# Storing the rows of a streamed weight chunk interleaved in DRAM

## The chip, the cores and the metric

One core of a Trainium2 chip runs the whole program. The metric is the device time of one execution in microseconds (us), median of several runs. Runs over 1.5% above the fastest of their kernel are marked slow.

## The reference, cut to what matters

The program computes two independent parts and puts them side by side. Part A is a long convolution by FFT; it fills most of the first 460 us and does not matter here. Part B is attention with a recurrent memory: 64 segments of 32 tokens, one after another, each projected by four weights of 1024 x 4096 (bf16).

```
for s in range(64):
    h = concat([mem, x[s]])                    # 40 rows
    q, k, v = h @ Wq, h @ Wk, h @ Wv           # 32 heads of 128
    o = softmax(mask(q k^T)) v @ Wo
    mem, out[s] = o[:8], o[8:]
```

The weights are 64 chunks of 512 KB. The program keeps 43 of them on the chip; the other 21 are streamed from DRAM again for every segment (two of them are parked elsewhere after the first segment, hence 64 x 19 + 2 = 1,218 loads).

## The kernel before

The streamed chunks are first copied into a DRAM tensor of their own, WS, one row of 4,096 bytes per partition. A ring of six SBUF tiles then receives them. Parts that do not matter are cut (`# ...`).

```python
RING = 6
PITCH = 2048
# ...
    def stream_src(ch):
        return WS[ring_order.index(ch), :, 0:2048]
# ...
    WS = dram.tile([len(ring_order), 128, PITCH], BF, name="WS")
# ...
                t = pw()
                nc.sync.dma_start(t[:], dram_chunk(ch))
                if ch in streamed:
                    nc.gpsimd.dma_start(stream_src(ch), t[:])
# ...
        for ch in ring_order:
            if ch[0] == 3:
                nc.gpsimd.dma_start(dst_view(stream_src(ch), ch), dram_chunk(ch))
# ...
    def slot():
        k = free.pop(0)
        t = ring.tile([128, 2048], BF, tag=f"wring{k}", name="wring")
        return k, t

    def fetch():
        if loads:
            s, ch = loads.pop(0)
            live[s, ch] = k, t = slot()
            nc.sync.dma_start(t[:], stream_src(ch))
```

The matmuls read a ring tile piece by piece; when one is done with, its slot goes back and the next load is issued on SP's queue.

## Time and profile before

| | before |
|---|---|
| time, median of 3 runs | 2193.94 us (2190.12 to 2201.51) |
| span of the profiled run | 2198.0 us |
| stream of weights, first to last issue | 461 to 2,175 us |
| loads of the stream | 1,218 of 512 KB |
| DMA rate in the stream, share of the 16 engines | 388 GB/s, 1.01 |
| 4,096-byte packets of SP's queue, 600 to 2,100 us | mean 168.3 ns, median 162 |
| TensorE waits for the stream | 188.2 us |

In the lines below, PE is TensorE (PEld its weight loads), DVE, ACT and POOL are the vector, scalar and GpSimd engines, and SP is the engine that issues the loads of the stream. A packet is one record of a DMA copy; in the stream it has 4,096 bytes, one row of one partition. The share of the DMA engines is the recorded time of their packets over the time of 16 engines; it can come out a little over 1.

The span is read in two stretches: before and after about 460 us. In the second, the DMA engines are always busy (share 1.01 from 600 to 2,100 us) and TensorE is not (1,213 of these 1,500 us), and what TensorE waits for most is the stream. Two lines of the page, the busy time of each engine and the granted TensorE clock in 40 slices (tenths of full speed):

```profile
PE 1721.9 (78%) x35607; PEld 927.7 (42%) x35636; DVE 884.2 (40%) x2702; ACT 638.6 (29%) x1118; POOL 412.2 (19%) x1103
...
PEclk9889997879999999999999999999999999999999
```

One more view, the tile view of wring, gives SP's time to issue a load (shortest, median, longest, in ns):

```profile
L658 SPq DMA_DIRECT2D wring<-WS x1218: 319/320/2190, 460.6 to 2175.1; - x174
```

### The profile page before, as it was taken

How to read it: one execution, taken by the hardware profiler on the slowest of the kernel's cores; microseconds unless marked ns; L12 is line 12 of the kernel's file. 1: busy time of each engine (PE TensorE's matmuls, PEld its weight loads, DVE VectorE, ACT ScalarE, POOL GpSimd, SP SyncE). 2: the span in 40 equal slices, each digit the busy share in tenths (PEclk: the TensorE clock that was granted, in tenths of full speed). 3: DMA queues.
4: the chain of work that ended last, by engine and by line, in shares of the span. 5: the costliest groups of instructions: out<-in, count | busy, mean ns of one | idle time of the engine just before them, and what ended most of it. 6: DMA issues, size and time to landing. Idle time of an engine off the chain costs nothing. (4 is left out here: it accounts for less than half of the span.)

```text
span 2198.0 us, 81500 instructions
## 1 busy us (share of the span) xinstructions
PE 1721.9 (78%) x35607; PEld 927.7 (42%) x35636; DVE 884.2 (40%) x2702; ACT 638.6 (29%) x1118; POOL 412.2 (19%) x1103
## 2 busy tenths in 40 slices
PE   4679975957777788878888888887887878888886
PEld 2233332424444444444444444444444444444444
DVE  8827853123333333333333333333333333333332
ACT  5845530112222222222222222222222222222222
POOL 5004331001111112111111111111111211211111
PEclk9889997879999999999999999999999999999999
DMA  9989989899999999999999999999999999999997
GB/s 322 345 291 342 318 238 325 275 346 390 386 380 378 381 374 390 385 378 395 391 392 395 391 393 393 392 397 365 396 392 387 394 390 376 388 392 388 390 385 273
DMA packets 294286, 807.80 MB, mean 368 GB/s; under 512 B 84940, under 2 KB 84972, under 8 KB 293927
## 3 DMA queue, kind: packets, MB, share of 16 engines
q1 hardware_dynamic: 263592, 738.36, 89.0%
q0 software_dynamic: 23536, 50.51, 6.8%
q10 hardware_dynamic: 6800, 13.72, 1.7%
q8 instruction: 279, 4.57, 0.9%
q14 instruction: 79, 0.65, 0.1%
HBM read 743.06 MB, written 62.39 MB: 366 GB/s over the span
## 5 line engine op out<-in xcount | busy, mean ns | idle before, releaser
L806 PEld LDWEIGHTS <-rec 128*32 128x32 bf16 x12351 | 324.2, 96 | 471.6 <-issue 255.0
L806 PE MATMUL acc<-wring,rec 128*32 128x512 bf16 (+1 forms) x3777 | 374.7, 385 | 136.0 <-DMA wring<-WS 122.1
L815 ACT CAST qkv_sb<-acc 128x512 bf16<-128x512 f32 x384 | 224.8, 585 | 676.2 <-PE acc L806 645.7
L806 PE MATMUL acc<-Wres,rec 128*32 128x512 bf16 x4864 | 394.9, 383 | 1.5 <-issue 1.4
L892 PEld LDWEIGHTS <-OT 128*32 128x32 bf16 x8192 | 217.8, 96 | 178.1 <-issue 151.6
L892 PE MATMUL yacc<-Wlate,OT 128*32 128x256 bf16 x5120 | 221.8, 274 | 13.0 <-issue 11.9
L892 PE MATMUL yacc<-wring,OT 128*32 128x256 bf16 x3072 | 153.9, 276 | 98.5 <-DMA wring<-WS 59.0
L806 PE MATMUL acc<-Wmid,rec 128*32 128x512 bf16 x3072 | 226.1, 383 | 0.5 <-issue 0.5
L752 PEld LDWEIGHTS <-OTB 128*16 128x16 bf16 x4096 | 104.5, 89 | 103.9 <-issue 94.0
L878 ACT CAST OT<-OTp 128x512 bf16<-128x512 f32 x128 | 74.9, 585 | 241.4 <-PE OTp L870 241.3
L707 POOL DMA_DIRECT2D rec<-REC x64 | 37.4, 584 | 566.6 <-issue 268.9
L908 DVE COPY KT<-tps 128x512 bf16<-128x512 bf16 x64 | 27.2, 424 | 289.1 <-PE tps L821 289.1
L879 DVE CAST OTB<-OTp 128x128 bf16<-128x128 f32 x128 | 37.3, 291 | 258.6 <-ACT OT L878 258.6
L647 DVE TENSOR_SCALAR wring<-OTp 128x384 int32<-128x384 int32 x126 | 112.2, 890 | 61.5 <-PE acc L806 54.2
L752 PE MATMUL SB<-Wlate,OTB 128*16 128x256 bf16 x2480 | 98.0, 277 | 35.4 <-DVE SB L743 19.3
L782 POOL COPY KT<-rec 128x128 bf16<-128x128 bf16 x128 | 38.6, 302 | 439.2 <-PE SB L830 430.9
L836 DVE TENSOR_REDUCE mx<-SB 128x5 f32<-128x200 f32 x128 | 47.1, 368 | 182.8 <-PE SB L830 182.8
L767 POOL DMA_DIRECT2D out_dram<-YB x128 | 73.1, 578 | 236.4 <-DVE YB L765 212.9
L752 PE MATMUL SB<-wring,OTB 128*16 128x256 bf16 x1488 | 78.8, 274 | 36.5 <-DVE SB L731 30.8
L821 PE MATMUL tps<-ident,qkv_sb 128*128 128x128 bf16 x1024 | 101.2, 221 | 7.8 <-DVE wring L647 0.2
L821 PEld LDWEIGHTS <-qkv_sb 128*128 128x128 bf16 x1024 | 62.7, 97 | 104.7 <-ACT qkv_sb L815 64.4
L556 PE MATMUL kb_ps<-XBT,pw 128*128 128x512 bf16 x314 | 87.7, 400 | 9.3 <-ACT XBT L512 7.6
(214 smaller groups left out, 2300.8 us busy)
## 6 DMA issues: line engine op xcount, KB each, us to landing
wring<-WS SPq DMA_DIRECT2D x1218, 512.0 KB, 7.3
rec<-REC POOLq DMA_DIRECT2D x64, 192.0 KB, 6.0
SK<-s_sb SPq DMA_DIRECT2D x16, 512.0 KB, 4.8
SU<-s_sb SPq DMA_DIRECT2D x16, 512.0 KB, 4.6
Ug<-SU SPq DMA_DIRECT2D x32, 256.0 KB, 6.1
Kg<-SK ACTq DMA_DIRECT2D x32, 256.0 KB, 5.5
REC<-stage SPq DMA_DIRECT2D x4, 2048.0 KB, 15.2
SZ<-zs SPq DMA_DIRECT2D x31, 256.0 KB, 3.0
```

The costliest lines, as they stand in the source:

```text
L556: nc.tensor.matmul(ps[:], lhsT=ws[kc][:, hl * 128:(hl + 1) * 128], rhs=XBT[:, kc].rearrange("p s t -> p (s t)"), start=(kc == 0), stop=(kc ...
L647: nc.vector.tensor_scalar(out=dst, in0=src, scalar1=0, scalar2=None, op0=ALU.bitwise_or)
L707: nc.gpsimd.dma_start(rec[:], REC[:, s, :])
L752: nc.tensor.matmul(self.acc[32 * dq:32 * dq + W, x - o:y - o], lhsT=self.OTB[:, c, 4 * g + i, :], rhs=r, start=first and not self.seeded, ...
L767: nc.gpsimd.dma_start(bass.AP(outb.tensor, outb.offset + (SEG * NB * self.b + NX) * 2048 + 256 * dq, [[2048 * SEG, NB], [2048, 8], [1, 256 ...
L782: nc.gpsimd.tensor_copy(KT[:, :, :, 32:40], KBs[:, 128 * g:128 * g + 128].rearrange("p (c i t) -> p i c t", c=4, i=4))
L806: nc.tensor.matmul(self.acc[32 * c:32 * c + 32, x - 512 * c:y - 512 * c], lhsT=hT[:, kc, :], rhs=r, start=(kc == 0 and x == 512 * c), stop ...
L815: nc.scalar.copy(sb[:], self.acc[:])
L821: nc.tensor.transpose(tp[:, i * 128:(i + 1) * 128], sb[:, i * 128:(i + 1) * 128], ident[:])
L836: nc.vector.tensor_reduce(out=mx[:], in_=S, op=ALU.max, axis=AX.X)
L878: nc.scalar.copy(OT[:], o_view[:, :, :, 0:32])
L892: nc.tensor.matmul(yacc[32 * dq:32 * dq + 32, x - o:y - o], lhsT=OT[:, c, i, :], rhs=r, start=(h == 0 and x == o), stop=(h == 31), tile_po ...
```

## The change

The intent: row `hi*8 + lo` is stored at place `lo*16 + hi`, so that the 16 rows with the same `lo` are neighbours in DRAM. That such an order is read faster was the assumption.

```diff
     def stream_src(ch):
-        return WS[ring_order.index(ch), :, 0:2048]
+        return WS[ring_order.index(ch), :, 0:2048].rearrange("(lo hi) c -> hi lo c", hi=16)
...
             if ch[0] == 3:
-                nc.gpsimd.dma_start(dst_view(stream_src(ch), ch), dram_chunk(ch))
+                for hh in range(2):
+                    nc.gpsimd.dma_start(stream_src(ch)[:, :, hh * 1024:(hh + 1) * 1024],
+                                        dram_chunk(ch)[:, hh, :].rearrange("(hi lo) d -> hi lo d", hi=16))
```

So the load of a chunk goes from 128x2048 to a source of 16x8x2048. Bytes, packets, matmuls and ring are the same.

## The prediction

The sum came to 3,660, 3,340 and 2,930 us; the packet times behind the first and the last are cut, and only 285 ns, from the early load X_sb, is left: 2,777 + 481 + 80 = 3,338 us. The prediction took 3,300 us, leaning to the upper half, and gave 86% to a slowdown, to between 2,500 and 3,700 us. Of the rivals, the first is that the new order is read faster, the second that nothing changes.

> **What bounds the kernel now.** I read the page's slices first. Up to slice 8 of 40 (about 460 us) the stages are mixed; from there to the end the pattern repeats for 64 segments, and DMA is at 9 tenths throughout.
>
> ```profile
> DMA  9989989899999999999999999999999999999997
> GB/s 322 345 291 342 318 238 325 275 346 390 386 380 378 381 374 390 385 378 395 391 392 395 391 393 393 392 397 365 396 392 387 394 390 376 388 392 388 390 385 273
> ```
>
> Second, the windows view of the steady part, cut into pieces. Columns: stretch, length, busy of PE, PEld, DVE, ACT, POOL with counts, granted clock, DMA share, GB/s. PE is busy 81%, the DMA engines all the time, at 388 GB/s.
>
> ```profile
> 600.00:2100.00 1500.00, 1212.78 (x29764) 691.69 (x29767) 544.52 (x1960) 385.02 (x729) 265.25 (x840) 0.99 1.01 388
> 900.00:1200.00 300.00, 242.35 (x5975) 140.10 (x5967) 108.11 (x388) 75.93 (x144) 55.34 (x174) 0.99 1.01 389
> ```
>
> Third, the waits of TensorE and what is issued. The streamed chunk wring<-WS (512 KB, 128 rows of 4,096 bytes, 1,218 times) is what the matmuls wait for, in the two lines below and in the chain of waits, where wring<-WS has 11% of the span, more than any other entry.
>
> ```profile
> PE acc L806 <- DMA wring<-WS: 122.1, 276, 2.0
> PE yacc L892 <- DMA wring<-WS: 59.0, 110, 1.6
> wring<-WS SPq DMA_DIRECT2D x1218, 512.0 KB, 7.3
> ```
>
> The tile view of wring puts the wait of PE for these landings at 188.2 us in all. 1,218 chunks of 524,288 bytes are 639 MB of the 808 MB moved. So the stream, 461 us to 2,175 us (first to last issue), is paced by DMA; SP often waits for a ring slot only because the 6 slots are all in flight or in use (a landing takes 7.3 us, over five chunks of the 1.41 us that one costs: 1,500 us / 1,064 chunks issued in the window above).
>
> Fourth, the DMA packet records (queue, start, duration, bytes). Between 600 and 2,100 us there are 136,186 packets of 4,096 bytes on SP's queue: quartile 159 ns, median 162, mean 168.3, 99th percentile 360. Packets of 2,048 bytes earlier have a floor of 84 ns. Two sizes give about 75 ns per 2,048 bytes and 9 ns fixed. Hence the **most that a better order of reading can give**: (168.3 - 159) x 136,186 / 16 = 79 us in that window, about 91 us for the whole stream, 4% of the time.
>
> [...] After the change the source is 16x8x2048 and the destination 128x1x2048 (the instruction listing of the changed kernel shows that form)[...]
>
> [...] in the first 20 us. Two kinds of SP load there don't have the plain 128-row form: Kx (112 rows, into partitions 1 to 112) and X_sb at L508, whose source is 16x8x1024 into 128x1x1024, exactly the changed form. Counting SP's 2,048-byte packets in order of issue, 12.6-13.4 us is mainly plain K rows, 13.6-14.8 Kx with some K, 16.2-17.4 plain K, 18.6-19.2 X_sb, 19.2-20.2 Kx.
>
> ```profile
> 12.60:13.40 0.80, 0.13 (x2) 0.13 (x3) 0.80 (x3) 0.00 (x0) 0.80 (x1) 1.00 1.07 405
> 13.60:14.80 1.20, 0.96 (x9) 0.81 (x8) 1.20 (x5) 1.06 (x2) 0.65 (x2) 1.00 1.07 271
> 16.20:17.40 1.20, 1.20 (x7) 0.48 (x6) 1.17 (x3) 1.20 (x2) 0.00 (x0) 1.00 1.06 389
> 18.60:19.20 0.60, 0.60 (x2) 0.00 (x0) 0.00 (x0) 0.00 (x0) 0.00 (x0) 1.00 1.05 239
> 19.20:20.20 1.00, 1.00 (x6) 0.42 (x5) 0.00 (x0) 0.88 (x1) 0.00 (x0) 1.00 1.04 256
> ```
>
> The engines are equally busy in all five (share 1.04 to 1.07), but move 405 and 389 GB/s in the plain form and 239 to 271 in the others. K and Kx read the same rows of HBM at the same 32 KiB pitch[...]. In X_sb's records an engine's first four packets take 84 to 100 ns, the next mostly 145 to 175[...].
>
> **The change part by part.**
> - Bytes, packets, matmuls, ring: as before. 1,218 loads of 128 rows of 4,096 bytes; nothing leaves the path.
> - Issue on SP: L508's X_sb took 590 and 669 ns to issue, the wring loads 320. Even 670 ns is half of the 1.41 us per chunk: hidden.
> - Stores of WS: 15 from pw in the new form, and 6 of Wo as 12 half ones. Six more POOL issues at 0.55 us are 3 us, and 15 stores of 512 KB, if slowed as below, add some 0.9 us each, 14 us, in stages where other work lies beside them. I count 0 to 15 us and leave it out.
> - HBM order: at most -91 us, from above; I expect under 20 of it.
> - [...] A packet's mean goes from 168.3 ns to:
>  [...]
>  - as the trace had it for X_sb: 405/239 = 1.69 times, 285 ns.
>
>  An engine writes 8 packets per chunk. With 1,218 chunks: [...] 285 gives 2,777, [...] today's 168.3 gives 1,640. Add 481 us outside the stream (2,198 less the 1,717 from 461 us to about 2,178) and about 80 us of engine time for the other packets in it (1,717 - 1,640): **3,660, 3,340 and 2,930 us**. I take 3,300. [...]
>
> At 285 ns a chunk costs about 2.35 us; PE needs 1,213 / 1,064 = 1.14 us per chunk, so all the added time is on the path.
>
> **The rivals.**
> - *Intended gain.* [...] For it: 1,370 packets (1%) are over 259 ns and hold about 41 us per engine of the 79. Against: the bulk sits at the floor. It makes 2,100 to 2,180 us.
> - *Nothing.* [...] For it: [...] X_sb is one load of 256 KB. Then about 2,190 us.
> - *HBM rather than SBUF slowed X_sb* (its "hi" rows lie 64 KiB apart). Then the changed layout, whose neighbours are 4 KiB apart, is not slow, and the result is one of the two above. Against: Kx is slow too, on rows that K reads at full rate.
> - *SP's issue as the new bound:* it would need over 1.41 us per load; nothing in the trace comes near.
>
> **Range and chances.** [...] Nothing: 9%. Gain over 2%: 5%. Range for 8 in 10: 2,500 to 3,700 us.
>
> **What would show it.** Right: the GB/s row falls to 210-280 from slice 9 on with the DMA share still at 1; the 4,096-byte packets on SP's queue take 240 to 320 ns at the median; time to landing rises from 7.3 us to 10-14; PE's wait for wring<-WS rises from 188 us to over 800; PE's busy time is unchanged. [...] Wrong: packets stay at 159 to 165 ns [...], or the tail over 360 ns vanishes and GB/s goes over 400 (the intended gain).

## The result, and the profile after

The changed kernel takes 3052.38 us (median of 4 runs, 3035.04 to 3070.68), the kernel before 2195.53 us in the same rounds. The ratio is 1.3903, with a 95% interval of 1.3806 to 1.4. Ratios here are the mean time of one kernel's fast runs over that of the other's of the same rounds, so not quite the ratio of the medians. The output is correct.

The page of the changed kernel, the same rows as before (engines, clock, DMA share, GB/s in 40 slices):

```profile
PE 2071.0 (68%) x35607; PEld 1061.5 (35%) x35636; DVE 885.6 (29%) x2702; ACT 638.3 (21%) x1118; POOL 414.8 (14%) x1109
...
PEclk9799886789888788787877877888788888888777
DMA  9998989999999999999999999999999999999997
GB/s 315 329 321 271 323 263 257 263 268 260 258 283 273 255 261 244 253 256 268 258 250 246 276 264 253 263 251 263 257 252 252 250 256 256 250 259 269 258 260 202
```

The DMA engines are as busy as before, but from the seventh slice on, where the stream begins, they move some 260 GB/s where it was 390 (share 1.03 and 259 GB/s in the windows below, against 1.01 and 388). That is the reading to keep: **a busy share says how long the engines had work, not how much they moved.** The windows view of the changed kernel, the first stretch and the stream (the granted clock, the DMA share and GB/s stand last):

```profile
0.00:460.00 460.00, 332.81 (x1624) 135.91 (x1653) 260.20 (x461) 197.51 (x285) 113.02 (x151) 0.89 0.92 304
...
600.00:2900.00 2300.00, 1547.84 (x30353) 827.11 (x30357) 557.58 (x1998) 392.04 (x742) 273.11 (x864) 0.82 1.03 259
```

The first stretch moves as much as before (304 against 305 GB/s in the same 460 us of the kernel before). All of the loss is in the stream. TensorE's waits in the changed kernel, then the chain that ended last, in the kernel before and in the changed one:

```profile
PE acc L808 <- DMA wring<-WS: 572.1, 631, 3.1
PE yacc L894 <- DMA wring<-WS: 214.8, 239, 2.5
```

```profile
DMA 11%; PE 3%; DVE 2%; issue 1%; ACT 0%; POOL 0%; SPq 0%; DVEq 0%; POOLq 0%; ACTq 0%
...
DMA 77%; PE 17%; issue 1%; ACT 1%; DVE 1%; SPq 1%; POOL 0%; ACTq 0%; DVEq 0%; POOLq 0%
```

The same two waits were 122.1 and 59.0 us. The two chain lines can't be set side by side as they stand: in the kernel before the chain could be followed back only to 1,811 us, the last 17% of the span, and DMA is 11 of these 17; in the changed kernel it is followed through nearly all of the span. Both say that DMA has most of what was followed; how much more, the waits say. From the tile view of wring, SP's issues in the changed kernel:

```profile
L660 SPq DMA_DIRECT2D wring<-WS x1218: 514/515/1807, 462.9 to 3031.7; - x174
```

Last, the packet records. SP's packets of 4,096 bytes in the stream (from 600 us to 2,100 before, to 2,900 after):

| | 5% | 25% | median | 75% | 95% | mean |
|---|---|---|---|---|---|---|
| before | 159 | 159 | 162 | 165 | 179 | 168.3 |
| changed | 182 | 232 | 261 | 286 | 316 | 259.2 |

The difference of the means, 90.9 ns, times 8 packets per engine and chunk (128 packets over 16 engines, on average), times 1,218 chunks, is 886 us. The measured difference of the medians is 857 us. The longer packets account for it.

### The profile page after: what moved, and what is told of

It reads as the page before. It is cut to its first block, busy times and chain, and to the rows that moved or that the text cites. A ratio compares the mean times of both kernels' runs of the same rounds, so it can differ in the third digit from the quotient of the medians.

```text
span 3058.8 us, 81509 instructions
## 1 busy us (share of the span) xinstructions
PE 2071.0 (68%) x35607; PEld 1061.5 (35%) x35636; DVE 885.6 (29%) x2702; ACT 638.3 (21%) x1118; POOL 414.8 (14%) x1109
## 4 chain that ended last, share of the span: by engine, by line
DMA 77%; PE 17%; issue 1%; ACT 1%; DVE 1%; SPq 1%; POOL 0%; ACTq 0%; DVEq 0%; POOLq 0%
DMA wring<-WS 73%; PE yacc L894 5%; PE acc L808 4%; PE kb_ps L556 3%; PE vb_ps L600 2%; PE SB L754 1%; DMA SK<-s_sb 1%; ACT s_sb L210 1%; DMA zt<-SZ 1%; DVE wring L649 1%; PE tps L823 0%; DMA Wres<-in_B_Wv_dram 0%; DMA Ug<-SU 0%; SPq L381 0%; PE z_ps L341 0%
## 5 line engine op out<-in xcount | busy, mean ns | idle before, releaser
L808 PE MATMUL acc<-wring,rec 128*32 128x512 bf16 (+1 forms) x3777 | 430.4, 436 | 576.1 <-DMA wring<-WS 572.1
L808 PEld LDWEIGHTS <-rec 128*32 128x32 bf16 x12351 | 350.5, 104 | 1047.9 <-issue 864.7
L808 PE MATMUL acc<-Wres,rec 128*32 128x512 bf16 x4864 | 446.8, 429 | 0.0
L894 PEld LDWEIGHTS <-OT 128*32 128x32 bf16 x8192 | 297.1, 122 | 339.2 <-issue 294.3
L894 PE MATMUL yacc<-wring,OT 128*32 128x256 bf16 x3072 | 198.6, 347 | 223.2 <-DMA wring<-WS 214.8
L894 PE MATMUL yacc<-Wlate,OT 128*32 128x256 bf16 x5120 | 305.2, 362 | 4.9 <-issue 4.1
L808 PE MATMUL acc<-Wmid,rec 128*32 128x512 bf16 x3072 | 297.3, 489 | 0.0
L754 PEld LDWEIGHTS <-OTB 128*16 128x16 bf16 x4096 | 117.9, 100 | 63.4 <-issue 45.0
L754 PE MATMUL SB<-wring,OTB 128*16 128x256 bf16 x1488 | 102.4, 351 | 1.6 <-issue 1.0
L950 ACT CAST Y<-yacc 128x256 bf16<-128x256 f32 x64 | 23.8, 372 | 366.3 <-PE yacc L894 353.6
```

The lines of the kernel that those rows point to most:

```text
L754: nc.tensor.matmul(self.acc[32 * dq:32 * dq + W, x - o:y - o], lhsT=self.OTB[:, c, 4 * g + i, :], rhs=r, start=first and not self.seeded, ...
L808: nc.tensor.matmul(self.acc[32 * c:32 * c + 32, x - 512 * c:y - 512 * c], lhsT=hT[:, kc, :], rhs=r, start=(kc == 0 and x == 512 * c), stop ...
L894: nc.tensor.matmul(yacc[32 * dq:32 * dq + 32, x - o:y - o], lhsT=OT[:, c, i, :], rhs=r, start=(h == 0 and x == o), stop=(h == 31), tile_po ...
```

## The experiments

**The theory.** The author explained the long packets by how a load of the new form is divided over the DMA engines and where these write. No record names an engine or the place where its data enter SBUF, so this was not shown. What the runs can test is that it is the form of the loads that makes packets long (16 in front on the DRAM side, or only 64 partitions). **The rivals:** the order of the rows in HBM (the chip's DRAM); something else in the new form (the number of its dimensions, or the longer issue on SP); the stores; a fixed cost of odd shapes.

The packet figures of all runs first (stream only; 4,096-byte packets, but 2,048 where it is said):

| run | time us | packets, median ns | quartiles | mean |
|---|---|---|---|---|
| before | 2193.94 | 162 | 159 to 165 | 168.3 |
| changed | 3052.38 | 261 | 232 to 286 | 259.2 |
| form only | 2996.18 (2 fast of 4) | 258 | 231 to 282 | 257.2 |
| loads only | 3035.5 (3 fast of 4) | 258 | 228 to 285 | 256.5 |
| stores only | 2199.72 | 162 | 159 to 165 | 168.2 |
| partition halves | 3197.69 | 274 | 248 to 295 | 272.9 |
| column halves (2,048 B) | 2281.65 | 85 | 84 to 89 | 90.6 |
| gap in the row (2,048 B) | 2299.43 | 85 | 84 to 89 | 90.7 |
| rows apart | 2197.14 | 162 | 159 to 165 | 168.6 |
| neighbours, plain form | 2196.14 | 161 | 159 to 165 | 169.0 |
| lower 64 partitions only | 2251.4 | 329 | 319 to 340 | 322.2 |
| half the columns only (2,048 B) | 1939.93 | 84 | 84 to 84 | 99.7 |
| changed, ring of 3 | 3542.1 (one run) | 286 | 255 to 311 | 281.8 |
| before, ring of 3 | 2911.12 (one run) | 159 | 159 to 159 | 192.4 |

### The form without the interleaving

```diff
-    WS = dram.tile([len(ring_order), 128, PITCH], BF, name="WS")
+    WS = dram.tile([len(ring_order), 16, 9, PITCH], BF, name="WS")
-        return WS[ring_order.index(ch), :, 0:2048].rearrange("(lo hi) c -> hi lo c", hi=16)
+        return WS[ring_order.index(ch), :, 0:8, :]
```

The edit is to the changed kernel. Rows are in natural order again; the ninth, unused row is to keep the two dimensions from being merged into one (SP's issue takes 515 ns here as in the change).

> The 16x8x2048 form without the interleaving: in DRAM each group of 8 rows lies in order, with one unused row after it so that the form isn't merged[...]. Theory [...]: as slow as the change, 2950 to 3150 us, packets of 4096 B at a mean of 245 to 275 ns. Rival (the interleaved order in HBM is what is slow): 2170 to 2230 us, packets near 168 ns.

Its two fast runs took 2975.6 and 3016.76 us, 1.3638 times the kernel before (1.3529 to 1.3747), with a correct result; the two marked slow took 3057.93 and 3068.01. The windows view of this run:

```profile
600.00:2100.00 1500.00, 1025.35 (x19990) 547.35 (x19990) 365.97 (x1305) 256.84 (x487) 179.24 (x569) 0.82 1.04 261
```

With the rows no longer neighbours the rate is 261 GB/s, as in the change. The interleaved order is not what is slow; the form is. Whether the order adds a little in this form stays open: the fast runs lie below those of the change (3,035 to 3,071 us), but all four together cover them.

### Loads alone, stores alone

Loads alone, an edit to the kernel before (storage as before, so the rows arrive in the wrong partitions; wrong):

```diff
-            nc.sync.dma_start(t[:], stream_src(ch))
+            nc.sync.dma_start(t[:], stream_src(ch).rearrange("(lo hi) c -> hi lo c", hi=16))
```

> The loads of the change alone: storage as before, loads in the interleaved 16x8x2048 form (wrong result on purpose). Theory: all of the loss is here, 3000 to 3100 us, packets near 259 ns. Rival: less than nine tenths of the loss, under 2960 us.

Stores alone, an edit to the changed kernel (wrong as well):

```diff
-            nc.sync.dma_start(t[:], stream_src(ch))
+            nc.sync.dma_start(t[:], WS[ring_order.index(ch), :, 0:2048])
```

> The stores of the change alone: interleaved storage, written as in the change, but the loads plain as before, so the rows come to the wrong partitions and the result is wrong on purpose. Theory: the stores cost 0 to 15 us, 2190 to 2215 us, packets of the stream near 168 ns. Rival (the stores' part matters): over 2240 us.

The loads alone took 3035.5 us (fast runs; ratio 1.3832, 1.3772 to 1.3892), 837 us over the kernel before in the same rounds (2198.24), where the change lost 857: all of the loss, within the spread of the runs. The stores alone took 2199.72 us, ratio 1.0018 (0.9989 to 1.0046): nothing that can be told from none.

### Two halves of the partitions, two halves of the columns

This pair asks whether packets get long without the new form. Both are edits to the kernel before, both give correct results, and both issue two plain transfers of 256 KB per chunk, in storage as before.

```diff
-            nc.sync.dma_start(t[:], stream_src(ch))
+            for a in (0, 64):
+                nc.sync.dma_start(t[a:a + 64, :], stream_src(ch)[a:a + 64, :])
```

> The kernel before, each chunk loaded by two plain transfers, partitions 0-63 and 64-127; storage, HBM order and plain form as before. Theory [...]: 2700 to 3600 us, packets 240 to 318 ns. Rivals (the three-dimensional form itself, or the order in HBM): within 5% of before, 2190 to 2300 us, packets near 168 ns.

```diff
-            nc.sync.dma_start(t[:], stream_src(ch))
+            for a in (0, 1024):
+                nc.sync.dma_start(t[:, a:a + 1024], stream_src(ch)[:, a:a + 1024])
```

> Control for the partition halves: two transfers a chunk as well, of all 128 partitions and half the columns. Theory [...] packets of 2048 B at 84 to 92 ns, twice as many, so 9 ns x 8 x 1218 = 88 us more of fixed cost: 2250 to 2320 us. Rival (issue time on SP, two issues of 320 ns a chunk or one of 515 ns, is what slows the change): as slow as the change, about 3000 us.

The partition halves took 3197.69 us (ratio 1.4547, 1.4515 to 1.458), the column halves 2281.65 us (1.0409, 1.0347 to 1.0472). The windows view of the partition halves, then that of the column halves:

```profile
600.00:2100.00 1500.00, 1003.48 (x18901) 456.71 (x18897) 349.62 (x1253) 243.63 (x464) 167.47 (x528) 0.79 1.03 246
```

```profile
600.00:2100.00 1500.00, 1242.16 (x28042) 675.42 (x28039) 513.29 (x1849) 362.54 (x687) 249.01 (x788) 0.99 1.03 366
```

246 against 366 GB/s, with equal bytes, equal numbers of transfers and the engines busy in both. SP's issues of the partition halves are longer:

```profile
L659 SPq DMA_DIRECT2D wring<-WS x2436: 444/445/1388, 455.9 to 3175.0; - x188
```

Two of these are 0.89 us per chunk, against 0.64 for the column halves; a chunk of the partition halves takes 2.23 us to come (2,719 us from first to last issue, over 1,218), with a DMA share of 1.03, so SP is not what limits them. The partition halves have neither the 16 in front nor a new order in HBM, and yet their packets have a median of 274 ns; what they have in common with the change was not shown. The column halves cost 85 us over the kernel before in the same rounds (2196.69), where the estimate of 9 ns fixed for each of 8 x 1,218 additional packets per engine (from the packets of 84 and 159 ns) had given 88.

### A gap in the row

```diff
-    WS = dram.tile([len(ring_order), 128, PITCH], BF, name="WS")
+    WS = dram.tile([len(ring_order), 128, 2, PITCH], BF, name="WS")
-        return WS[ring_order.index(ch), :, 0:2048]
+        return WS[ring_order.index(ch), :, :, 0:1024]
-            nc.sync.dma_start(t[:], stream_src(ch))
+            nc.sync.dma_start(t[:].rearrange("p (hh d) -> p hh d", hh=2), stream_src(ch))
...                                                     # the stores in the same form
```

> A three-dimensional form that keeps 128 as slowest dimension: in DRAM a gap in the middle of each row, 128x2x1024, one transfer per chunk. Theory ([...] not the number of dimensions or the issue time): packets of 2048 B at 84 to 92 ns, 2250 to 2320 us, like the column halves. Rival (three-dimensional forms cost by themselves): over 2500 us.

2299.43 us (1.048, 1.0443 to 1.0517), correct. The tile view of wring in this run:

```profile
L658 SPq DMA_DIRECT2D wring<-WS x1218: 517/518/2098, 458.8 to 2275.5; - x174
```

So this form costs SP as much per issue as the change (515 ns), and yet the time is that of the column halves. So three dimensions and the longer issue cost little in this form: the two ratios' intervals overlap, and the medians over their own rounds differ by 17 us (102 and 85).

### What the order in HBM is worth

Rows of a chunk 84 KiB apart, plain form, correct:

```diff
-    WS = dram.tile([len(ring_order), 128, PITCH], BF, name="WS")
+    WS = dram.tile([128, len(ring_order), PITCH], BF, name="WS")
-        return WS[ring_order.index(ch), :, 0:2048]
+        return WS[:, ring_order.index(ch), 0:2048]
```

> The kernel before with the rows of one chunk 84 KiB apart in DRAM (row-major over the 21 chunks), plain form. Theory [...]: 2170 to 2230 us, packets 159 to 172 ns. Rival (what the 16 engines read at a time in HBM matters by more than 5%): outside 2085 to 2305 us.

Neighbours in the plain form: rows overlap at a pitch of 1 KiB, so that partitions 4 apart are 4 KiB apart (wrong data). It is not quite the order of the change: the rows overlap, and which of them are read at one time is not in the records.

```diff
-            nc.sync.dma_start(t[:], stream_src(ch))
+            src = stream_src(ch)
+            nc.sync.dma_start(t[:], bass.AP(src.tensor, src.offset, [[512, 128], [1, 2048]]))
```

> [...] plain 128x2048 loads with a row pitch of 1 KiB in DRAM, overlapping rows (wrong data on purpose), [...] over 131 KiB per chunk. Theory (no loss in HBM to repair): packets 159 to 172 ns at the mean, 2150 to 2220 us. Rival (the intention is right, only the form spoiled it): packets at 159 to 162 ns at the mean, 2090 to 2140 us.

Ratios 1.0003 (0.9986 to 1.0019) and 1.0 (0.9975 to 1.0025). The windows view of the neighbours, near in the plain form to the access that the change was after:

```profile
600.00:2100.00 1500.00, 1202.20 (x29548) 684.36 (x29548) 540.70 (x1947) 383.10 (x724) 265.46 (x839) 1.00 1.01 386
```

It moves what the kernel before does (388). With rows 4, 84 and 1 KiB apart giving the same time (ratios within 0.25%), no gain from the order in HBM shows in this kernel. What makes the 1% of long packets (99th percentile 382 ns here, 360 before) was not found.

### Half of each chunk only

A direct test of 64 partitions against half the columns. Edits to the kernel before: the ring's tiles are allocated once, and after the first six chunks only half of each is loaded, the lower 64 partitions in one run, half the columns in the other. Half the bytes are gone in both; both results are wrong. That the tiles are allocated once, which both runs share and the kernel before does not, was not tested by itself.

```diff
-        t = ring.tile([128, 2048], BF, tag=f"wring{k}", name="wring")
+        t = slots[k]
...
-            nc.sync.dma_start(t[:], stream_src(ch))
+                nc.sync.dma_start(t[0:64, :], stream_src(ch)[0:64, :])       # one run
+                nc.sync.dma_start(t[:, 0:1024], stream_src(ch)[:, 0:1024])   # the other
```

> After the first six chunks only partitions 0-63 of each chunk are loaded, plain form, half the bytes (wrong result on purpose). Theory: [...] median 300 to 325 ns, where the change's median is 261; quarter to quarter narrow (under 30 ns). [...] 2030 to 2200 us although half the bytes are gone. Rival ([...] a fixed cost of odd forms): packets 159 to 200 ns.

> Control: the same half of the bytes, but as half the columns of all 128 partitions (wrong result on purpose). Theory: packets of 2048 B at 84 to 90 ns, DMA no longer the bound, 188 us of waits for the stream go: 1980 to 2040 us. Rival for the run above (time falls with the bytes whatever the partitions): both of these runs take the same time within 1%.

With half the bytes over 64 partitions the program took 2251.4 us, **more** than with all of them (1.0258, 1.0224 to 1.0293); with half the columns it took 1939.93 us (0.8838, 0.8816 to 0.886). Windows view of the lower 64 partitions, then of half the columns:

```profile
600.00:2100.00 1500.00, 1195.10 (x28602) 677.90 (x28598) 522.83 (x1880) 367.92 (x701) 255.22 (x809) 0.96 0.97 194
```

```profile
600.00:1900.00 1300.00, 1139.90 (x30304) 674.67 (x30307) 554.07 (x1996) 391.47 (x741) 271.01 (x857) 0.99 0.74 237
```

In the first the engines are busy (share 0.97) with 194 GB/s; the second moves 237 with a share of 0.74, and TensorE waits 6.0 us for its stream. (The waits alone would mislead here: in the first, TensorE's waits for the stream are 118 us, less than the 188 of the kernel before, and 131 us of its waits are put down to nothing that the profile shows.) The packets of the first are nearly all alike, quartiles 319 and 340, twice those of the kernel before (159 and 165). The change lies between the two, with packets from 182 to 316 ns (5% to 95%). One test was not run: another set of 64 partitions, 32 to 95. So for the runs with 64 partitions the rival "fewer than 128 partitions in a transfer" is not excluded; for the change it is, since its loads write all 128 and have a median of 261 ns. Why the packets are long was not shown in either. The expectations missed in two numbers: the packets are 329 ns and not at most 325, and the time is 2251 us and not at most 2200; and half the columns saved 258 us where the wait of 188 us had given 158 to 218. The waits that TensorE's view puts down to the stream are thus not all that the stream cost; which others went was not followed.

### A ring of three

```diff
-RING = 6
+RING = 3
```

> The changed kernel with 3 ring slots in place of 6[...]. [...] median of the 4096 B packets 285 to 318 ns. If [...] the form has a fixed cost of 1.55 times: median 250 to 270 ns as with 6 slots. Time over 3052 us in both.

> Control for the changed kernel with 3 slots: the kernel before with 3 slots. [...] median 159 to 166 ns. If a short ring lengthens packets in any form: median over 175 ns. Time 2250 to 2700 us in both, as the landings are waited for more.

The median of the changed kernel's packets rose from 261 to 286 ns, at the very edge of the higher of the two ranges (285 to 318); that of the kernel before fell from 162 to 159. By the medians a short ring does not lengthen packets in the plain form. By the means it does: they rose by 24 ns in the kernel before (168.3 to 192.4, the 95th percentile from 179 to 406) and by 23 in the changed one (259.2 to 281.8). In the plain form a few packets got much longer, in the changed form the whole distribution moved. What made either longer was not shown: the records do not name the engine of a packet, and the long packets of the plain form were not explained. The time of the kernel before with three slots, 2911 us, was outside what was expected (2250 to 2700), against 2193.94 with six: the ring's depth matters more to it than was thought.

## Why the prediction was right

3,300 us was predicted, with 2,500 to 3,700; 3052.38 us was measured.

- *What bounds the kernel: DMA, in the stream.* Right: the change touches the loads alone, and 857 us followed. Half the columns took 258 us off.
- *The form of the loads decides.* Right, but the records do not show which engine copies which partitions. What the runs show: both kernels whose loads have 16 as slowest dimension and the right data (the change, form only), and the loads alone, have medians of 258 to 261 ns; both that keep 128 (column halves, gap in the row) have 2,048-byte packets at 85.
- *What makes the packets long.* The records show no cause. Measured are medians of 329 ns with the lower 64 partitions only, 274 with the partition halves, 261 with the change, and 162 before.
- *The size.* This is the term that was mis-sized. The prediction leaned on 285 ns, taken from 0.6 us of one early load (405/239 = 1.69 times). That window cut the load: counted in order of start, X_sb's 128 packets begin at 18.26 us, the first 64 with a mean of 91 ns and the last 64 with 150, and the window holds most of the second half and little more. The whole load has a mean of 120 ns where the K rows before it had 88, 1.37 times, which would have given an estimate of 230 ns. So this load gave no safe size either way. (That it was "an engine's first four packets" is inferred from the order; no record names the engine.) Over the stream the mean is 259.2 ns, 1.54 times, with a spread of 182 to 316 ns from the 5th to the 95th percentile. With that mean, the prediction's own sum is 8 x 259.2 x 1,218 = 2,526, plus 80 and 481, 3,087 us, 1.1% over the measurement. The reason for leaning above 1.5 is cut; no run shows it, and the stream came out near 1.5 (1.54).
- *The order in HBM, under 20 us.* Right as far as tested; the plain form measured none (1.0, within 0.25%). A slip in the rival's favour: 1,370 packets are over 358 ns; over 259 ns there are 2,235, and the 41 us are theirs.
- *Issue on SP and the stores, hidden.* Right: 515 ns per issue, and 2199.72 us with the stores alone.
- *The chain, 11% for wring<-WS.* Read too weakly: it is 11 of the 17% that could be followed.
- *GB/s of 210 to 280, share still 1.* Right: 244 to 283 from slice 9 to the last but one, share 1.03.
- *PE's wait over 800 us, time to landing 10 to 14 us.* The wait is 800.7 us in the tile view. The landings could not be paired in the changed kernel's profile; in the form-only run they take 11.8 us.
- *PE's busy time unchanged.* Wrong: 1721.9 us became 2071.0, with a granted clock of 0.82 in the stream where it was 0.99. That it did not lengthen the time is argued, not tested: TensorE's 1,548 us of the 2,300 in the stream are 1.42 us per chunk (139,331 packets / 128 = 1,088 chunks), and a chunk takes 2.11 us to come.

## What to carry to other kernels

Before rearranging the DRAM side of a transfer, look at its form: in these runs a first dimension of 128 on both sides kept the short packets (85 ns for 2,048 bytes even with a third dimension), and a tidier order in HBM with 16 in front cost 39%. Read GB/s beside the DMA share, and the durations of packets of one size beside both: they told, 20 us into the trace of the kernel before, what a load of the new form would do in kind, if not in size (239 GB/s at a share of 1.05, against 405 at 1.07). And when a short stretch gives the size of an effect, take the whole transfer and let the range carry it, not the centre: 1.69 times in 0.6 us was 1.37 over that load and 1.54 over the stream.
